# A11 B11 of a feed-forward kernel's second matrix product made by seven quarter products, from the third unit on

## The chip, the cores and the metric

The kernel runs on one core of a Trainium2 chip. The metric is the device time of one execution in microseconds (us), as the median of several runs. The kernel before took 959.35 us (median of 3 runs, 957.83 to 960.07). The profiled execution spans 957.3 us, and all positions in the traces are microseconds from the start of that span.

## The reference, cut to what matters

```python
kv  = einsum('bhsd,bhse->bhde', k, v)             # linear attention, 8 x 8 heads, 576 x 64
o   = einsum('bhsd,bhde->bhse', q, kv)
o   = o / sqrt(mean(o*o, -1) + 1e-6) * g_norm
x   = o.transpose(0, 2, 1, 3).reshape(4608, 512)
h   = x @ w_in                                    # 512 -> 2048
g   = s * relu(h)**2 + b
out = g @ w_out                                   # 2048 -> 512
```

All of it is fp32. The change touches only the last line, `g @ w_out`. The kernel keeps r = relu(h)**2 as its hidden value and puts the rest into the evacuation: the result is s * (r @ w_out) plus one constant row, the column sums of w_out times b (`b_row`, line 329, whose left and right halves are `b1` and `b2`).

## The kernel before, in words

The 4608 tokens are worked in nine units of 512 tokens (`u` = 0 to 8; the loop is at line 1152). In a unit comes first the **first product** (`mm1`, line 562), which gives the hidden values transposed, in four steps `s` = 0 to 3 of 4 x 128 hidden rows, and then the **second product** (`mm2`, line 646). Beside the second product, the attention of the next unit's tokens is made in small pieces (`turn`, `product`, `norm`, `turn_x`, lines 388 to 472).

Both products use a scheme with seven block products in place of eight (Winograd's form of Strassen's). A matrix is cut into four blocks; products 1 to 7 are made of blocks and of sums of blocks, and the partial results are added. In the second product the hidden values are A (`a11`: first 256 tokens, first half of the hidden rows; `a12`: the same tokens, second half; `a21` and `a22`: the other 256 tokens), and w_out is B (512-column rows cut into halves of 256). A11 B11 is product 1, A12 B21 is product 2, and so on (`G_OF`, line 644, tells which A goes with which number).

A plain block product (`product`, line 650) runs for each of two 128-token groups `j` over 8 hidden blocks `f`: each call is one matmul with 128 x 128 weights and 256 columns, accumulated in a PSUM bank. In the traces one fp32 call is two weight loads and two matmul records, so such a product has 16 records for each `j`.

From the third unit on (`u` > 1), three of the seven, products 2, 7 and 4 (`TWICE`, line 274), are made by the scheme **a second time** (`second_level`, line 678): the block is cut again, into quarters, and seven quarter products of 4 calls each (8 records) with 128 columns stand for the plain product's two groups. They need four sums of quarters of A, made on VectorE (`sums`, line 688), and the sums of quarters of B, which are made once, in unit 1 (`parts_of_w`, line 664), stored in HBM (`w3_dram`, line 275) and loaded again in each unit.

The quarter products run in the order 1, 2, 6, 7, 5, 3, 4 (`ORDER`, line 618). They share PSUM banks, and the way they do is needed below. Quarter product 1 starts the bank called "x" (line 716); `keep` (line 711) reads it on VectorE into a small tile `r1`; then product 6 **adds to the same bank** (line 724), `r2` is read from it, and product 5 adds to it again (line 731), then product 3. Product 7 starts the bank "y", and product 4 adds to it. Product 2 has the bank "z".

PSUM pool `ps_f` has two banks with the tag "x", two with the tag "y" and one "z". In `second_level` both "x" and "y" are taken from the tag "y" (line 704).

The order of the work is written out by hand: the program runs under a manual schedule (line 87), so each engine runs its instructions in the order in which the Python code issues them. For `u` > 1 that order is in `first` (line 924) and `second` (line 929). Around the end of the first product it is: `x5` of step 3 (its bank is copied by ScalarE, then VectorE adds and squares it: line 590), then `first` (two transposes `turn`, and `x1(0)`, half of product 1), then the last two blocks of the first product, `x3` and `y4` of step 3 (lines 1197 to 1199), then `second`: two of the four sums for product 2, `x1(1)`, and the quarter products of product 2. `attend(0)` (line 920) is the attention product of the next unit's first 128 tokens with its norm, and `x6_of(0)` (line 896) the next plain product; it reads `a11` after `s2` (line 798) has overwritten it with a sum.

Weights of the second product come through a ring of seven tiles (`late["ring"]`, line 997), loaded on SyncE's queue by `pump` (line 628), two tiles a call.

Of the kernel before, what the change touches and what calls it, by code (L numbers as in the profile page):

```python
# [15 lines left out]
def kernel(  # L16
# [211 lines left out]
    def add(o, a, b):  # L228
        nc.vector.tensor_tensor(out=o, in0=a, in1=b, op=ALU.add)  # L229
# [41 lines left out]


    w2_dram = [dram.tile([P, FC // 2, HN], FP32, name=f"w2_{i}") for i in range(8)]
    TWICE = (2, 7, 4)
    w3_dram = {
        i: dram.tile([P, 7, FC // 4, P], FP32, name=f"w3_{i}") for i in TWICE
    }
# [232 lines left out]
    def bank_of(key, tag, bufs=2):  # L510
        bank[key] = ps_f.tile([P, 2, TB], FP32, name=f"{tag}_ps", tag=tag, bufs=bufs)
        return bank[key]
# [133 lines left out]
    def mm2(u, att=None):  # L646
# [3 lines left out]
        def product(i, j, ps, first):  # L650
            for f in range(FC // 2):
                s, b = divmod(f, 2)
                w2 = W2_AT[i][:, f] if u == 0 else ring[u, i, f // 4][:, f % 4]
                matmul(
                    ps, ga[G_OF[i], s][:, b, j * P : j * P + P], w2,
                    first and f == 0, f == FC // 2 - 1,
                )

        def scaled(o, ps, other):
            nc.vector.scalar_tensor_tensor(o, ps, s_col, other, ALU.mult, ALU.add)  # L660
# [14 lines left out]
            for n, t in enumerate((y11, y21, t2, t3, t1, y22, t4)):  # L675
                nc.sync.dma_start(out=w3_dram[i][:, n], in_=t)

        def second_level(i, other, to):


            a, t, r = {}, {}, {}
            cols = [slice(q * P, q * P + P) for q in range(2)]

            def quarter(j, h):
                g = g_pair[G_OF[i], h].rearrange("p s b t -> p (s b) t")
                return g[:, :, j * P : j * P + P]

            def sums(which=(5, 6, 7, 3)):
                x11, x12, x21, x22 = (quarter(j, h) for j in range(2) for h in range(2))
                a.update({1: x11, 2: x12, 4: x22})  # L690
                for m in which:
                    a[m] = late["sub"].tile([P, FC // 4, P], FP32, name="sub", tag="sub")
                    if m == 5:
                        add(a[5], x21, x22)
                    elif m == 6:
                        sub(a[6], a[5], x11)
                    elif m == 7:
                        sub(a[7], x11, x21)
                    else:
                        sub(a[3], x12, a[6])  # L700

            def go(m, bank, first):
                if first:
                    t[bank] = bank_of((bank, i), "z" if bank == "z" else "y", 1 if bank == "z" else 2)
                    t[bank] = t[bank].rearrange("p b n -> p (b n)")[:, :P]
                n = ORDER.index(m)
                w = ring[u, i, n // 2][:, n % 2]
                for f in range(FC // 4):
                    matmul(t[bank], a[m][:, f], w[:, f], first and f == 0, f == FC // 4 - 1)

            def keep(name, j, q):
                r[name] = late["tmp"].tile([P, P], FP32, name="r", tag="r")
                scaled(r[name], t["x"], other(j, cols[q]))

            def m1():
                go(1, "x", True)
                keep("r1", 0, 0)

            def m2():
                go(2, "z", True)  # L720
                scaled(to(0, cols[0]), t["z"], r["r1"])

            def m6():
                go(6, "x", False)
                keep("r2", 1, 0)

            def m7():
                go(7, "y", True)

            def m5():  # L730
                go(5, "x", False)
                keep("r4", 1, 1)
                scaled(to(1, cols[1]), t["y"], r["r4"])

            def m3():
                go(3, "x", False)
                scaled(to(0, cols[1]), t["x"], other(0, cols[1]))

            def m4():
                go(4, "y", False)  # L740
                scaled(to(1, cols[0]), t["y"], r["r2"])

            return {"sums": sums, 1: m1, 2: m2, 6: m6, 7: m7, 5: m5, 3: m3, 4: m4}
# [7 lines left out]
        def rows(name, j):  # L751
            if (name, j) not in st:
                st[name, j] = outp.tile([P, DM], FP32, name=name, tag=name)
            return st[name, j]
# [15 lines left out]
        def x1(j):  # L770
            st["x", j] = half(("x", j), "x")
            product(1, j, st["x", j], True)
            if u > 0:
                part("r1", j, st["x", j], b1)
# [49 lines left out]

        def x3(j):
            product(3, j, st["x", j], False)
            scaled(rows("o1", j)[:, HN:], st["x", j], b2 if u > 0 else st["o1", j][:, HN:])
            store("o1", j, 4 * u + j)

        def y4(j):  # L830
# [40 lines left out]
            ]  # L871
        if u == 1:
            return [
                lambda: x1(0),
                seq(lambda: x1(1), lambda: pump(2), s2),
                seq(lambda: z2(0), lambda: parts_of_w(2)),
                seq(lambda: z2(1), lambda: pump(2), s4),
                lambda: x6(0),
                seq(lambda: x6(1), lambda: pump(2)),
                seq(lambda: y7(0), lambda: parts_of_w(7)),  # L880
                seq(lambda: y7(1), lambda: pump(2)),
                lambda: x5(0),
                seq(lambda: x5(1), lambda: pump(2)),
                lambda: x3(0),
                seq(lambda: x3(1), lambda: pump(2)),
                seq(lambda: y4(0), lambda: parts_of_w(4)),
                seq(lambda: y4(1), lambda: pump(2)),
            ]

        p2 = second_level(2, lambda j, q: st["r1", j][:, q], lambda j, q: rows("o1", j)[:, q])  # L890
        p7 = second_level(
            7, lambda j, q: b2[:, q], lambda j, q: rows("o2", j)[:, HN:][:, q]
        )
        p4 = second_level(4, lambda j, q: st["r2", j][:, q], lambda j, q: rows("o2", j)[:, q])

        def x6_of(j):
            product(6, j, st["x", j], False)
            part("r2", j, st["x", j], b_12)

        def x5_of(j):  # L900
# [1 line left out]

        def with_7(j):

            right = st["o2", j][:, HN:]
            add(st["r2", j], st["r2", j], right)
            scaled(right, st["x", j], right)
            if last(j):
                store("o2", j, 4 * u + 2 + j, slice(HN, DM))

# [10 lines left out]
            product_q[c]()  # L921
            norm[c]()

        def first():
            turn[0]()
            turn[1]()
            x1(0)

        def second():
            p2["sums"]((5, 6))  # L930
            x1(1)
            pump(2)
            p2[1]()
            p2["sums"]((7,))
            p2[2]()
            p2["sums"]((3,))
            p2[6]()
            s2((0, 1))
            p2[7]()
            p2[5]()  # L940
            s2((2, 3))
            pump(2)
            attend(0)
            p7["sums"]()
            x6_of(0)
            p2[3]()
            p2[4]()
            pump(2)
            attend(1)
            turn_x[0]()  # L950
            turn[2]()
            x6_of(1)
            pump(2)
            p7[1]()
            s4((0,))
            p7[2]()
            p7[6]()
            s4((1,))
            p7[7]()
            s4((2,))  # L960
            p7[5]()
            s4((3,))
            pump(2)
            attend(2)
            turn_x[1]()
            turn[3]()
            x5_of(0)
            p7[3]()
            with_7(0)
            p7[4]()  # L970
            pump(2)
            attend(3)
            turn_x[2]()
            x5_of(1)
            with_7(1)
            turn_x[3]()
            pump(2)
            p4["sums"]()
            x3(0)
            for m in (1, 2, 6, 7, 5):  # L980
                p4[m]()
            pump(2)
            x_sums_next[0]()
            x3(1)
            pump(2)
            y4_of(0, 3)
            y4_of(1, 4)
            pump(2)

        return [first, second]  # L990


    NU = FC // 2
# [158 lines left out]
    for u in range(U):  # L1152
# [11 lines left out]
            slots += [a["x6"], a["y7"], a["x5"]]  # L1164
        if u == 0:
            first_unit()
        for n, slot in enumerate(slots):
            slot()
            if u == 1 and n in (1, 3, 5):
                for sums in sums_w_in((n + 1) // 2):  # L1170
                    sums()
            if u in kv_due and n == 12:
                kv_product(kv_due[u])
            elif u + 1 in kv_due and n == 14:
                for i in range(2):
                    load_kv(kv_due[u + 1], i, late["kv"], tag="kv")
        side = side_of(u)
        second = mm2(u, side if u > 1 else None)
        if u > 1:
            side = {}  # L1180
        for n, slot in enumerate(second):
# [55 lines left out]
```

## Time and profile before

| | busy us | share of the 957.3 us |
|---|---|---|
| TensorE matmuls (PE) | 944.8 | 99% |
| TensorE weight loads (PEld, beside the matmuls) | 839.6 | 88% |
| VectorE (DVE) | 580.6 | 61% |
| ScalarE (ACT) | 194.5 | 20% |
| DMA, all queues | 143.73 MB moved, 150 GB/s | |

The granted TensorE clock is 0.997 over the span. Units 2 to 8 are alike and take about 102 us each: `x1(0)` starts at 294.42, 396.43 and so on.

How to read the profile: a row of a timeline has a start, a duration, the engine, the line of the kernel, the operation, the tile written and the tiles read, and the shape. Several instructions in a row that are alike are merged and counted (x16). Line 90 is the matmul helper, so tiles tell the products apart: `x_ps`, `y_ps` and `z_ps` are the banks, `w_sb` the ring of weights, `a` any hidden block, `sub` a sum for the second level. A merged PE row lasts until its last matmul has drained; the pace is the distance from its start to the start of the next row. Idle time of an engine that is not the bound costs nothing.

### The profile page before, as it was taken

What the parts mean: (1) busy time and instruction counts of PE and PEld (TensorE: products, weight loads), DVE (VectorE), ACT (ScalarE), POOL (GpSimd) and SP (SyncE); (2) the same over time, 40 slices, a digit from 0 to 9 for tenths busy, and PEclk for the clock granted to TensorE, in tenths of its full rate; (3) what the DMA queues carried; (4) which work ended last, traced back from release to release, by engine and by line L of the source; (5) the groups of instructions that cost most, each with busy time, mean ns of one, the idle gap of its engine ahead of it and who ended that gap; (6) DMA issues with size and microseconds to landing.
All of it is one profiled execution on the core that took longest, in us unless ns stands there. A gap on an engine that the chain in (4) does not pass through costs nothing.

```text
span 957.3 us, 16744 instructions
## 1 busy us (share of the span) xinstructions
PE 944.8 (99%) x6934; PEld 839.6 (88%) x6934; DVE 580.6 (61%) x1019; ACT 194.5 (20%) x366; POOL 6.7 (1%) x18
## 2 busy tenths in 40 slices
PE   7999999999999999999999999999999999999997
PEld 7888888888888898899889988989898988998897
DVE  2789667465537754586358745774467556864463
ACT  2684131201120112112211212021202111111100
POOL 2000000000000000000000000000000000000000
PEclk9999999999999999999999999999999999999999
DMA  9598729567743565165444565266215630552063
GB/s 240 193 323 242 256 78 278 110 186 215 209 98 101 180 185 120 45 203 161 111 107 152 169 167 117 91 197 180 31 59 180 194 64 19 191 175 68 1 207 101
DMA packets 127532, 143.73 MB, mean 150 GB/s; under 512 B 76256, under 2 KB 87264, under 8 KB 127328
## 3 DMA queue, kind: packets, MB, share of 16 engines
q1 hardware_dynamic: 124352, 140.88, 51.3%
q10 hardware_dynamic: 2784, 1.77, 0.8%
q8 instruction: 55, 0.90, 0.4%
q14 instruction: 21, 0.17, 0.1%
q0 software_dynamic: 320, 0.00, 0.0%
HBM read 120.33 MB, written 22.28 MB: 149 GB/s over the span
## 4 chain that ended last, share of the span: by engine, by line
PE 96%; DMA 2%; DVE 1%; ACT 1%; issue 0%; SPq 0%; ACTq 0%; DVEq 0%
PE x_ps L90 51%; PE y_ps L90 30%; PE z_ps L90 8%; PE x_ps L421 3%; PE kv_ps L359 2%; DMA w_raw<-in_moe_w_in_dram 1%; DMA kv_sb<-in_k_dram 1%; PE qT_ps L400 0%; DVE xn L440 0%; DVE xT L464 0%; ACT xT L470 0%; ACT w_raw L209 0%; SPq L102 0%; ACT w_raw L204 0%; DVE wb L224 0%
## 5 line engine op out<-in xcount | busy, mean ns | idle before, releaser
L90 PE MATMUL x_ps<-w_sb,a 128*128 128x256 f32 x768 | 174.7, 381 | 0.0
L90 PEld LDWEIGHTS x_ps<-w_sb,a 128*128 128x128 f32 x768 | 144.0, 190 | 21.5 <-issue 2.8
L568 ACT COPY r<-x_ps 128x512 f32<-128x512 f32 x96 | 56.2, 585 | 332.0 <-PE x_ps L90 325.3
L90 PE MATMUL y_ps<-xs,wb 128*128 128x256 f32 x512 | 121.0, 379 | 0.0
L90 PE MATMUL x_ps<-xs,ws 128*128 128x256 f32 x512 | 120.9, 379 | 0.0
L229 DVE TENSOR_TENSOR a<-y_ps,r 128x512 f32<-128x512 f32 x64 | 44.0, 688 | 122.2 <-ACT r L568 122.2
L90 PEld LDWEIGHTS x_ps<-xs,ws 128*128 128x128 f32 x512 | 97.3, 190 | 13.2
L90 PEld LDWEIGHTS y_ps<-xs,wb 128*128 128x128 f32 x512 | 97.3, 190 | 13.2
L90 PE MATMUL x_ps<-xT,wa 128*128 128x256 f32 x384 | 89.6, 380 | 0.1
L90 PE MATMUL y_ps<-w_sb,sub 128*128 128x128 f32 x672 | 81.8, 275 | 0.0
L90 PEld LDWEIGHTS x_ps<-xT,wa 128*128 128x128 f32 x384 | 72.3, 190 | 10.2 <-ACT xT L470 0.5
L90 PEld LDWEIGHTS y_ps<-w_sb,sub 128*128 128x128 f32 x672 | 80.0, 192 | 1.1
L523 DVE SCALAR_TENSOR_TENSOR a<-a 128x512 f32<-128x512 f32 x96 | 66.5, 692 | 3.3
L601 DVE TENSOR_TENSOR a<-a 128x512 f32<-128x512 f32 x32 | 22.1, 691 | 75.9 <-ACT a L600 75.9
L90 PE MATMUL y_ps<-w_sb,a 128*128 128x128 f32 (+1 forms) x416 | 62.2, 295 | 0.0
L90 PE MATMUL x_ps<-xT,ws 128*128 128x256 f32 x256 | 61.1, 381 | 0.0
L90 PE MATMUL z_ps<-xT,wa 128*128 128x256 f32 x256 | 60.5, 379 | 0.0
L90 PEld LDWEIGHTS y_ps<-w_sb,a 128*128 128x128 f32 x416 | 57.5, 191 | 3.2 <-issue 0.2
L90 PE MATMUL x_ps<-w_sb,s 128*128 128x256 f32 x256 | 59.1, 384 | 0.0
L90 PEld LDWEIGHTS x_ps<-w_sb,s 128*128 128x128 f32 x256 | 47.4, 190 | 8.4 <-issue 2.4
L430 ACT ACTIVATE xn<-x_ps 128x512 f32<-128x512 f32 x34 | 20.3, 597 | 168.4 <-PE x_ps L421 165.9
L90 PEld LDWEIGHTS z_ps<-xT,wa 128*128 128x128 f32 x256 | 48.6, 190 | 6.6
(122 smaller groups left out, 994.9 us busy)
## 6 DMA issues: line engine op xcount, KB each, us to landing
w_sb<-w SPq DMA_DIRECT2D x133, 512.0 KB, 4.7
kv_sb<-in_k_dram SPq DMA_DIRECT2D x30, 288.0 KB, 5.3
kv_sb<-in_v_dram SPq DMA_DIRECT2D x30, 288.0 KB, 6.1
w_raw<-in_moe_w_in_dram SPq DMA_DIRECT2D x8, 1024.0 KB, 7.2
w_raw<-in_moe_w_out_dram SPq DMA_DIRECT2D x8, 1024.0 KB, 5.3
out_dram<-o SPq DMA_DIRECT2D x104, 64.0 KB, 1.7
w_sb<-w SPq DMA_DIRECT2D x21, 256.0 KB, 2.8
q_sb<-in_q_dram SPq DMA_DIRECT2D x144, 32.0 KB, 2.1
```

Source lines behind the costliest of these rows:

```text
L90: nc.tensor.matmul(o, lhsT=lhsT, rhs=rhs, start=start, stop=stop, skip_group_check=True)
L229: nc.vector.tensor_tensor(out=o, in0=a, in1=b, op=ALU.add)
L359: nc.tensor.matmul(ps[r][l * HB : l * HB + HB, i, :], lhsT=kv[rows, 0, l, j, :], rhs=kv[rows, 1, l, j, :], start=(j == 0), stop=(j == R - 1),)
L421: nc.tensor.matmul(ps[32 * p : 32 * p + 32, w, :], lhsT=st["qT"][:, p, 32 * w : 32 * w + 32], rhs=bd_kv[(b if w < 2 else b1) % 2][:, p, :] ...
L430: nc.scalar.activation(st["xn"], st["x"], AF.Square)
L523: nc.vector.scalar_tensor_tensor(t, t, 0.0, t, ALU.max, ALU.mult)
L568: nc.scalar.copy(st[name], src)
L601: nc.vector.tensor_mul(t, t, t)
```

## The change

Product 1 joins `TWICE`: from the third unit on, A11 B11 too is made of seven quarter products. Its purpose is to make that product with fewer multiplications on TensorE. The quarter products 1, 2, 6, 7 and 5 stand before the last two blocks (`x3`, `y4`) of the first product, and 3 and 4 after them; the four sums are issued ahead of `x5` of the last step.

Because A11 B11 is then no longer in a PSUM bank that products 6, 5 and 3 could add to, it is kept (with `b2`) in the right half of the output rows `o1`, and goes from there into the evacuations of products 2, 7 and 3. Product 6 starts its own bank, and the left half of the rows gets `b_12` = `b1` - `b2` by two more additions. The attention product of the next unit (`product_q[0]`) moves ahead of product 2's quarter products, and its norm stays behind them.

```diff
-    TWICE = (2, 7, 4)
+    TWICE = (1, 2, 7, 4)
@@ second_level
-        def second_level(i, other, to):
+        def second_level(i, other, to, x_tag="y"):
...
-                    t[bank] = bank_of((bank, i), "z" if bank == "z" else "y", 1 if bank == "z" else 2)
+                    tag = {"x": x_tag}.get(bank, bank)
+                    t[bank] = bank_of((bank, i), tag, 1 if tag == "z" else 2)
@@ x3
-            scaled(rows("o1", j)[:, HN:], st["x", j], b2 if u > 0 else st["o1", j][:, HN:])
+            scaled(rows("o1", j)[:, HN:], st["x", j], b2 if u == 1 else st["o1", j][:, HN:])
@@ unit 1
-                lambda: x1(0),
+                seq(lambda: x1(0), lambda: parts_of_w(1)),
@@ units 2 to 8
+        def right(name, j, q=slice(0, HN)):
+            return rows(name, j)[:, HN:][:, q]
+
-        p2 = second_level(2, lambda j, q: st["r1", j][:, q], lambda j, q: rows("o1", j)[:, q])
+        p1 = second_level(1, lambda j, q: b2[:, q], lambda j, q: right("o1", j, q), "x")
+        p2 = second_level(2, lambda j, q: right("o1", j, q), lambda j, q: rows("o1", j)[:, q])
...
-            7, lambda j, q: b2[:, q], lambda j, q: rows("o2", j)[:, HN:][:, q]
+            7, lambda j, q: right("o1", j, q), lambda j, q: right("o2", j, q)
...
         def x6_of(j):
-            product(6, j, st["x", j], False)
+            st["x", j] = half(("x", j), "x")
+            product(6, j, st["x", j], True)
...
-        def first():
+        def sums_ahead():
+            p1["sums"]()
             turn[0]()
             turn[1]()
-            x1(0)
+
+        def first():
+            for m in (1, 2, 6, 7, 5):
+                p1[m]()
+            pump(2)
 
         def second():
+            p1[3]()
             p2["sums"]((5, 6))
-            x1(1)
+            p1[4]()
             pump(2)
+            product_q[0]()
             p2[1]()
             p2["sums"]((7,))
             p2[2]()
...
-            attend(0)
+            norm[0]()
             p7["sums"]()
             x6_of(0)
             p2[3]()
             p2[4]()
+            for j in range(2):
+                left = rows("o1", j)[:, :HN]
+                add(left, left, b_12)
@@ the loop over the units
+        side = side_of(u)
+        second = mm2(u, side if u > 1 else None)
+        if u > 1:
+            ahead, *second = second
         for n, slot in enumerate(slots):
             slot()
+            if u > 1 and n == len(slots) - 2:
+                ahead()
```

More of the change, by code (lines that the diff above doesn't have):

```diff
@@ L903, in with_7 @@
         def with_7(j):
-            right = st["o2", j][:, HN:]
-            add(st["r2", j], st["r2", j], right)
-            scaled(right, st["x", j], right)
+            to = right("o2", j)
+            add(st["r2", j], st["r2", j], to)
+            scaled(to, st["x", j], to)
             if last(j):
@@ L988, in second @@
             pump(2)
-        return [first, second]
+        return [sums_ahead, first, second]
     NU = FC // 2
@@ L1176 @@
                     load_kv(kv_due[u + 1], i, late["kv"], tag="kv")
-        side = side_of(u)
-        second = mm2(u, side if u > 1 else None)
         if u > 1:
```

## The prediction

> **What bounds the kernel now.** I read the page's busy table first, then the chain that ended last:
>
> ```profile
> PE 944.8 (99%) x6934; PEld 839.6 (88%) x6934; DVE 580.6 (61%) x1019; ACT 194.5 (20%) x366; POOL 6.7 (1%) x18
> ```
> ```profile
> PE 96%; DMA 2%; DVE 1%; ACT 1%; issue 0%; SPq 0%; ACTq 0%; DVEq 0%
> ```
>
> TensorE sets the time; nothing else is within a third of it on average. Where TensorE isn't held up, a change is worth its matmul time; an idle gap made on TensorE is paid in full. So I looked at the seam that the change rebuilds, in the timeline of unit 3 (start, duration, engine):
>
> ```profile
> 394.70 1.89 PE L90 MATMUL x_ps<-xs,ws 128*128 128x256 f32 x8
> 396.43 3.62 PE L90 MATMUL x_ps<-w_sb,a 128*128 128x256 f32 x16
> 396.68 0.59 ACT L568 COPY r<-x_ps 128x512 f32<-128x512 f32 x1 [2.92 <-PE x_ps L90]
> 397.30 0.69 DVE L229 TENSOR_TENSOR a<-y_ps,r 128x512 f32<-128x512 f32 x1 [3.88 <-ACT r L568]
> 398.03 0.69 DVE L523 SCALAR_TENSOR_TENSOR a<-a 128x512 f32<-128x512 f32 x1
> 398.63 1.30 DVE L391 STREAM_TRANSPOSE qT<-q_sb 128x512 f32<-128x512 f32 x2
> 399.88 1.89 PE L90 MATMUL x_ps<-xT,ws 128*128 128x256 f32 x8
> 401.61 1.89 PE L90 MATMUL y_ps<-xs,wb 128*128 128x256 f32 x8
> ...
> 403.33 3.62 PE L90 MATMUL x_ps<-w_sb,a 128*128 128x256 f32 x16
> ...
> 405.21 0.69 DVE L523 SCALAR_TENSOR_TENSOR a<-a 128x512 f32<-128x512 f32 x1
> ...
> 405.94 0.69 DVE L229 TENSOR_TENSOR sub<-a,a 128x512 f32<-128x512 f32 x1
> 406.67 0.69 DVE L232 TENSOR_TENSOR sub<-sub,a 128x512 f32<-128x512 f32 x1
> 406.79 1.05 PE L90 MATMUL y_ps<-w_sb,a 128*128 128x128 f32 x8
> ...
> 407.27 0.48 DVE L660 SCALAR_TENSOR_TENSOR or<-x_ps,s_col,b_row 128x256 f32<-128x256 f32 x1
> 407.68 1.06 PE L90 MATMUL z_ps<-w_sb,a 128*128 128x128 f32 x8
> 407.88 0.35 DVE L660 SCALAR_TENSOR_TENSOR r<-y_ps,s_col,or 128x128 f32<-128x128 f32 x1
> 408.15 0.68 DVE L232 TENSOR_TENSOR sub<-a 128x512 f32<-128x512 f32 x1
> 408.57 2.84 PE L90 MATMUL y_ps<-w_sb,sub 128*128 128x128 f32 x24
> ```
>
> In order: `x5` of the last step (394.70), `x1(0)`, `x3`, `y4` (401.61), `x1(1)` (403.33), then quarter products 1, 2 and 6, 7, 5 of product 2. Two things are to be seen. TensorE never pauses. And VectorE, 61% busy on average, works without a pause from 404.5 on: r1, read from bank "x", ends at 408.23, only 0.34 before quarter product 6 adds to that bank (408.57).
>
> [...] The rows agree: both engines keep the code's order. So a late evacuation stops the matmul that needs its bank and all matmuls behind it. [...] here the data alone forces it, since r1 must be read before 6 is added. [...] this trace has 690. [...] here 350, which I use.
>
> **The change, part by part.**
>
> *Matmul work.* 16 records of 256 columns take 3.45 (396.43 to 399.88), so `x1(0)` and `x1(1)` cost 6.90. In their place come 56 records of 128 columns. In product 2, 8 take 0.89 or 0.90 (406.79, 407.68, 408.57), hence 56 take 6.26. Saved: 0.64 a unit, in seven units 4.5 us. That is all there is to gain.
>
> *VectorE order.* A started 128x512 operation holds the next one back 0.60 (0.73 if the next needs its result), a 128x128 one 0.27 (0.39). PSUM is readable 0.20 after the next TensorE row begins (401.61, ScalarE's 401.81). VectorE's end reaches TensorE's weight load 0.06 later (near the start a copy ends at 24.65, the load is at 24.71); from its restart a matmul may lose 0 to 0.2 more.
>
> *First wait, quarter product 6 of product 1.* I keep unit 3's clock. Products 1 and 2 run 396.43 to 398.22, where 6 wants bank "x". It must wait for r1, which stands on VectorE behind the evacuation of `x5`: ScalarE's copy ends 397.27, the add is at 397.30, the square at 398.03, so r1 starts 398.63 and ends 398.98. Moving the sums ahead doesn't help, since it is ScalarE's copy that the add waits for. (The four sums and two transposes start about 393.35 and end about 397.2, in the 3.88 that VectorE idles now: no cost.) Product 6 starts about 399.09, a wait of 0.87; bounds 0.80 and 1.0. Behind it stand all of TensorE's matmuls. Before, `x1(0)` covered this: 3.45 of matmul that needed nothing from VectorE.
>
> *`x3`, `y4`.* r2 and r4 then follow in time; ScalarE's and VectorE's work on `x3` and `y4` keeps its distance to them. Call the end of `y4` Y (403.33 before). The square of `y4` starts at Y+1.88, as before.
>
> *Second wait, quarter product 6 of product 2.* TensorE after Y: 3 and 4 of product 1 (1.79), the attention product (0.1 to switch, 1.01), quarter products 1 and 2 (1.79): 6 is wanted at Y+4.68; before it came at Y+5.24. VectorE from the square: evacuation of 3 at Y+2.48, two sums at 2.75 and 3.48, evacuation of 4 at 4.08, the attention's row sum of squares at 4.35, r1 at 4.98, done at 5.33. Product 6 starts about Y+5.40: a wait of 0.72, bounds 0.65 and 0.9. The sum for 7 ends at 5.93, in time for Y+6.3. TensorE's path has become 0.56 shorter and VectorE's row before r1 0.78 longer (r1 began at Y+4.55, waiting 0.13 for its turn).
>
> *Third.* `x6_of(0)` now follows directly, without the attention product's 1.01 as cover. It starts Y+8.1 and needs the third block of `s2` at Y+9.8; this is done at Y+9.62. With the weight load ahead that is 0 to 0.25; I take 0.1.
>
> *A unit:* 0.87 + 0.72 + 0.1 - 0.64 = +1.05; six units (2 to 7): +6.3.
>
> *The last unit* has no attention. Product 6 of product 2 is wanted at Y+3.6 and r1, without the row sum before it, ends at 4.70: 1.15, with some 0.05 for a bank that `y4`'s add frees at Y+1.85. 0.87 + 1.2 - 0.64 = +1.4.
>
> *Costed at nothing:* the weights of product 1 in unit 1 (four VectorE operations, 2.7; VectorE idles there before 196.00 and again before 200.55, and `z2` needs their followers after 203), their seven stores (like those of product 2, in the next 3 to 6 us, and the two ring slots are wanted again only for `x6`, 10 us later), the larger loads (4 tiles for 2; four quarter tiles of product 1 arrive during the 45 us of the first product; 512 KB land in 4.7 and the tightest, the second tile of `x6`, has about 8), and the two additions by `b_12` (0.8, under `x6_of(1)`). Banks of `x6_of` are long free.
>
> Sum: 959.35 + 6.3 + 1.4 = 967.0.
>
> **The rivals.** *A, as above:* 967.0; low bounds (0.80 + 0.65 - 0.64 = 0.8 a unit, 1.2 in the last) give 965.3, high ones (1.0 + 0.9 + 0.25 - 0.64 = 1.5, last 1.9) 970.3.
>
> *B, the matmuls decide (faster):* the evacuations keep up and 4.5 is saved: 954.9. For it: products 2, 7 and 4 run by this scheme with no pause now. Against it: in products 7 and 4, VectorE had caught up when they began; here both r1 stand behind a full row of 128x512 work.
>
> *C, one wait only:* the first or the second is hidden by something that I mis-ordered. Then a unit gives -0.64 + 0.1 + 0.72 or 0.87, so +0.2 to +0.3: over seven units 960.6 to 961.7.
>
> *D, more waits:* VectorE stays behind into product 7, or a ring tile is late. In my row r1 of product 7 is still waiting for TensorE, 0.3 ahead of need. 0.7 more a unit: 972.
>
> **How the numbers follow.** A 0.77, B 0.09, C 0.08, D 0.06. The likeliest gives 967.0. The range takes A's bounds and the runs' own spread of 1 us: 964 to 971. Faster by over 0.2% (1.9 us): B, and a little for a case in which both waits shrink, 0.10. Within: most of C, 0.06. Slower: the rest, 0.84.
>
> **What would show it.** In the profile after: a hole of about 0.9 in TensorE's row before the 24 records of quarter products 6, 7, 5 of product 1, ended by VectorE's r (line of `scaled`), and one of about 0.7 before those of product 2, ended likewise; in the last unit 1.1 there. 56 records of 128 columns in 6.26 apart from the holes. The four sums ahead of `x5` without cost. Wrong it would be if product 6 ran on at once (then r1 was read earlier than I order it), if the holes lay elsewhere, or if the matmuls' pace differed from product 2's.

## The result, and the profile after

The changed kernel took 964.85 us (median of 6 runs, 964.15 to 966.49) against 958.59 us of the kernel before in the same comparison: a ratio of 1.0064, with a 95% interval of 1.0045 to 1.0082. (Ratios below are formed in the same way, each against the kernel before as it ran beside that version.) It is slower by 6.3 us, less than 1% but clear of the noise. The two profiled executions span 964.3 and 957.3 us. The forecast was 967.0 us, 7.65 us slower than the 959.35 us known then.

The page of the changed kernel, its line of busy times:

```profile
PE 943.5 (98%) x7102; PEld 840.8 (87%) x7102; DVE 612.1 (63%) x1100; ACT 194.3 (20%) x366; POOL 6.7 (1%) x18
```

TensorE has 168 records more (7 units, 56 for 32) and a little less busy time (944.8 us before), and yet the span is longer: the time went into gaps. VectorE has 31.5 us more work. The view of the waits tells who made the gaps (engine and what it wrote, whom it waited for, us in total, times, longest):

```profile
PEld x_ps L90 <- DVE r L660: 6.0, 7, 0.9
...
PE x_ps L90 <- DVE r L660: 4.6, 7, 0.7
PEld y_ps L90 <- DVE r L660: 4.4, 7, 1.0
...
PE y_ps L90 <- DVE r L660: 3.1, 7, 0.8
```

None of these four is in the waits of the kernel before. Each comes seven times, once in each of units 2 to 8: TensorE waits for the tile `r`, an evacuation by VectorE, once before it writes bank "x" and once before bank "y". The timeline of unit 3 shows the first of the two, at the place that answers to 394.70 to 403.33 before (unit 3 starts 1.2 us later in this execution):

```profile
395.88 1.89 PE L90 MATMUL x_ps<-xs,ws 128*128 128x256 f32 x8
...
397.61 1.05 PE L90 MATMUL x_ps<-w_sb,a 128*128 128x128 f32 x8
397.87 0.58 ACT L568 COPY r<-x_ps 128x512 f32<-128x512 f32 x1 [2.92 <-PE x_ps L90]
...
398.49 0.69 DVE L229 TENSOR_TENSOR a<-y_ps,r 128x512 f32<-128x512 f32 x1
398.50 1.06 PE L90 MATMUL z_ps<-w_sb,a 128*128 128x128 f32 x8
399.21 0.69 DVE L523 SCALAR_TENSOR_TENSOR a<-a 128x512 f32<-128x512 f32 x1
...
399.82 0.34 DVE L660 SCALAR_TENSOR_TENSOR r<-x_ps,s_col,b_row 128x128 f32<-128x128 f32 x1
...
400.22 1.16 PE L90 MATMUL x_ps<-w_sb,sub 128*128 128x128 f32 x8 [0.66 <-DVE r L660]
...
401.22 1.06 PE L90 MATMUL y_ps<-w_sb,sub 128*128 128x128 f32 x8
```

Quarter product 1 starts at 397.61, 2 at 398.50; 6 was due 0.89 later, at 399.39, and starts at 400.22, after r1, which VectorE could begin only at 399.82, behind the copy, add and square of `x5`. The row's own 0.66 is counted from the modelled end of the matmuls before; the start is late by 0.83.

The second, at the head of product 2 (the 32 records of line 421 are the attention product):

```profile
408.34 1.08 PE L421 MATMUL x_ps<-bd_kv,qT 128*32 128x128 f32 x32
...
409.35 1.16 PE L90 MATMUL y_ps<-w_sb,a 128*128 128x128 f32 x8
...
410.34 1.06 PE L90 MATMUL z_ps<-w_sb,a 128*128 128x128 f32 x8
...
410.80 0.68 DVE L432 TENSOR_REDUCE ss<-xn 128x8 f32<-128x512 f32 x1
411.39 0.34 DVE L660 SCALAR_TENSOR_TENSOR r<-y_ps,s_col,o 128x128 f32<-128x128 f32 x1
...
411.79 2.94 PE L90 MATMUL y_ps<-w_sb,sub 128*128 128x128 f32 x24 [0.39 <-DVE r L660]
...
414.57 3.62 PE L90 MATMUL x_ps<-w_sb,a 128*128 128x256 f32 x16
...
418.02 1.05 PE L90 MATMUL y_ps<-w_sb,sub 128*128 128x128 f32 x8
```

Due at 411.23, started at 411.79: 0.56 late, behind r1, which here stands behind the row sum of squares of the attention (410.80).

Each of units 2 to 7 became 0.93 us longer: quarter product 1 of unit 2 starts 0.26 later than `x1(0)` did (294.68 for 294.42), that of unit 8 5.81 later (907.39 for 901.58), which is 5.55 over six units. The last unit became 1.55 longer. With the 0.26 from before unit 2, and 0.4 won back behind the last matmuls, where the stores end, this is the 7.0 between the spans.

### The profile page after: what moved, and what is told of

It reads as the page before. It is cut to its first block, busy times and chain, and to the rows that moved or that the text cites. A ratio compares the mean times of both kernels' runs of the same rounds, so it can differ in the third digit from the quotient of the medians.

```text
span 964.3 us, 17222 instructions
## 1 busy us (share of the span) xinstructions
PE 943.5 (98%) x7102; PEld 840.8 (87%) x7102; DVE 612.1 (63%) x1100; ACT 194.3 (20%) x366; POOL 6.7 (1%) x18
## 5 line engine op out<-in xcount | busy, mean ns | idle before, releaser
L90 PE MATMUL x_ps<-w_sb,a 128*128 128x256 f32 (+1 forms) x600 | 130.9, 371 | 0.0
L90 PEld LDWEIGHTS x_ps<-w_sb,a 128*128 128x128 f32 x600 | 108.6, 190 | 15.2 <-issue 1.6
L90 PE MATMUL y_ps<-w_sb,sub 128*128 128x128 f32 x728 | 90.0, 276 | 3.1 <-DVE r L660 3.1
L90 PEld LDWEIGHTS y_ps<-w_sb,sub 128*128 128x128 f32 x728 | 86.8, 192 | 5.5 <-DVE r L660 4.4
L90 PEld LDWEIGHTS x_ps<-xT,wa 128*128 128x128 f32 x384 | 72.3, 190 | 10.2 <-ACT xT L470 0.5
L90 PE MATMUL y_ps<-w_sb,a 128*128 128x128 f32 (+1 forms) x472 | 70.3, 294 | 0.0
L90 PEld LDWEIGHTS y_ps<-w_sb,a 128*128 128x128 f32 x472 | 63.8, 191 | 4.2 <-DVE o L660 1.2
L90 PEld LDWEIGHTS x_ps<-xT,ws 128*128 128x128 f32 x256 | 47.6, 190 | 6.3
```

The lines of the kernel that those rows point to most:

```text
L90: nc.tensor.matmul(o, lhsT=lhsT, rhs=rhs, start=start, stop=stop, skip_group_check=True)
```

## The experiments

The theory at this point: the matmul work fell as forecast, and two separate waits for an evacuation, each placed late in VectorE's order of work (r1 at 399.82 behind the square at 399.21, and at 411.39 behind the row sum at 410.80), cost more. The rival that is hard to tell apart from a trace: VectorE as a whole is the bound of this stretch (its pauses between 406 and 424 are few and short in either kernel, none above 0.8 us), and a gap that is closed opens again further on.

**The first wait alone.** Quarter product 1, and with it r1, goes ahead of `x5`; 6 comes before 2, so that r2 is not delayed in turn. Nothing is left out.

```diff
         def sums_ahead():
             p1["sums"]()
+            p1[1]()
             turn[0]()
...
-            for m in (1, 2, 6, 7, 5):
+            for m in (6, 2, 7, 5):
                 p1[m]()
```

> Edit: quarter product 1 of A11 B11 and its evacuation r1 are issued before x5 of the first product (after the four sums), and the rest runs 6, 2, 7, 5; only the order changes. Theory (two separate waits for evacuations that stand late on VectorE): r1 is read before the evacuation of x5, so the hole of 0.82 us before quarter product 6 of product 1 and about 0.1 for the restart go away in seven units, 6.4 us in all: about 958.4 us, with the second hole (0.56 in units 2 to 7, 0.97 in the last) as it was. Rival (VectorE as a whole is the bound of the seam, and a hole closed opens again further on): about 964.5 us as in the changed kernel, the second hole grown to about 1.4.

Measured: 958.11 us (13 runs), ratio to the kernel before 0.9998 (0.9990 to 1.0006). That is what the theory gave (958.4). Its timeline of unit 3:

```profile
394.31 1.05 PE L90 MATMUL x_ps<-w_sb,a 128*128 128x128 f32 x8
...
395.20 1.89 PE L90 MATMUL x_ps<-xs,ws 128*128 128x256 f32 x8
395.48 0.34 DVE L660 SCALAR_TENSOR_TENSOR r<-x_ps,s_col,b_row 128x128 f32<-128x128 f32 x1
...
396.93 1.05 PE L90 MATMUL x_ps<-w_sb,sub 128*128 128x128 f32 x8
```

and its row of the second wait:

```profile
PE y_ps L90 <- DVE r L660: 3.1, 7, 0.8
```

r1 is done at 395.82, more than a microsecond before 6 needs its bank (396.93), and no gap is left there. The second wait is as it was, in sum (3.1) and in its longest (0.8). So the first wait did not move on. Its cost was 6.3 us by the two ratios (1.0064 less 0.9998, each known to 0.1 or 0.2%), and by the trace of the changed kernel 7 x 0.94 = 6.6 (0.83 late and 0.11 for the restart, the first step after the gap taking 1.00 where the others take 0.89). That is as much as the whole slowdown: the saving of matmul work and the second wait are left, and nearly cancel.

**The second wait alone.** The row sum of squares is split from the attention product (`False` leaves it to a later call; the lines that define `sum_sq_of` are not shown) and issued by `sum_sq_of` after the sums of `s2`. Nothing is left out. The helper's line 660 is line 667 in this version and the later ones with it.

```diff
-            product_q[0]()
+            product_q[0](False)
             p2[1]()
...
             s2((2, 3))
             pump(2)
+            if att:
+                sum_sq_of[4 * u + 4]()
             norm[0]()
```

> Edit: the attention product stays where it is, but its row sum of squares on VectorE (0.68 us) is issued behind the second pair of s2 sums instead of ahead of r1 of product 2. Theory: r1 of product 2 ends 0.63 us earlier, the hole of 0.56 before quarter product 6 of product 2 closes in units 2 to 7 (with its restart 0.6 to 0.7 each, 4 us in all): about 961 us; the last unit, without attention, keeps its 0.97. Rival (VectorE as a whole is the bound): the hole opens again before x6 or in product 7, about 964.5 us.

Measured: 963.94 us (5 runs), ratio to before 1.0057 (1.0045 to 1.0069); 0.7 less than the changed kernel by the ratios and 1.4 by the profiled spans (962.9 for 964.3), where the theory gave 4. The two intervals overlap, so the trace has to tell what happened. Here the theory fell short. Its timeline of unit 3:

```profile
410.35 0.34 DVE L667 SCALAR_TENSOR_TENSOR r<-y_ps,s_col,o 128x128 f32<-128x128 f32 x1
...
410.78 2.90 PE L90 MATMUL y_ps<-w_sb,sub 128*128 128x128 f32 x24
...
424.31 1.06 PE L90 MATMUL z_ps<-w_sb,a 128*128 128x128 f32 x8
...
425.12 0.34 DVE L667 SCALAR_TENSOR_TENSOR r<-y_ps,s_col,o 128x128 f32<-128x128 f32 x1
...
425.50 1.64 PEld L90 LDWEIGHTS y_ps<-w_sb,sub 128*128 128x128 f32 x14 [0.33 <-DVE r L667]
```

The gap of product 2 is closed (410.78), but a new one stands 15 us later, before quarter product 6 of **product 7**: due at 425.20, it starts at 425.50, again after an r1. VectorE had carried its backlog that far: of the 0.66 won in a unit (0.56 and about 0.1 of restart) 0.4 was given back.

**Both.** The two edits together.

> Edits of the two runs before together. Theory: both holes go and the matmul saving of 0.64 us a unit is left, less about 0.8 in the last unit: about 954.5 us, faster than the kernel before by 4 us (0.4%). Rival (VectorE as a whole is the bound): little under 962 us, with new holes further on, first before quarter product 6 of product 7.

Measured: 956.77 us (14 runs), ratio to before 0.9991 (0.9982 to 0.9999). Its view of waits has one row for the gaps that `r` makes:

```profile
PEld y_ps L90 <- DVE r L667: 2.9, 7, 1.0
```

In units 2 to 7 the two early gaps are gone and product 7's is there, with 0.31 and its restart of 0.1; the longest, 1.0, is the second gap of the last unit, which has no row sum to move. 6 x 0.41 = 2.5 us, and the 954.5 of the theory with 2.5 is 957.0, close to what was measured. So both theories hold in part: the first wait was a matter of order alone, the second one hid a true backlog of VectorE, of less than half a microsecond, which ended at product 7.

**The backlog taken away.** The two additions of `b_12`, 0.75 us together, stood right in that backlog; they are needed only when the rows are stored. From the version with both edits they move to behind quarter product 4 of product 7, where VectorE idled 1.03 us in the kernel before (434.17 to 435.20).

```diff
             p2[4]()
-            for j in range(2):
-                left = rows("o1", j)[:, :HN]
-                add(left, left, b_12)
...
             p7[4]()
+            for j in range(2):
+                left = rows("o1", j)[:, :HN]
+                add(left, left, b_12)
```

> Edit: as in the run with both edits, and the two additions of b_12 (0.75 us on VectorE) are issued behind quarter product 4 of product 7, where VectorE idled 1.03 us in the kernel before, instead of ahead of the second attention product. Theory: the hole of 0.31 us that the two edits left before quarter product 6 of product 7 is made by VectorE's backlog there, and r1 of product 7 comes 0.4 to 0.6 us earlier: it closes, with its restart 0.4 us in each of six units: 956.8 - 2.4 = 954.4 us; only the last unit keeps its hole of 0.97. Rival (VectorE's backlog moves on once more): about 956.8 us with a hole further on.

Measured: 955.33 us (13 runs), ratio to before 0.9966 (0.9957 to 0.9975). This version beats both kernels: by medians it is 2.7 us under the 958.02 of the kernel before beside it, by the ratio 3.3. Of the gaps made by `r` one is left in its view of waits, that of the last unit:

```profile
PEld y_ps L90 <- DVE r L667: 1.0, 1, 1.0
...
PE y_ps L90 <- DVE r L667: 0.8, 1, 0.8
```

**One sum more out of the way.** The sum for quarter product 7 of product 2 needs no block of the last step; on top of the edit before, it is issued before `x3`, where VectorE idled 1.6 us in the version with both edits (399.22 to 400.84).

```diff
             for m in (6, 2, 7, 5):
                 p1[m]()
+            p2["sums"]((7,))
...
             p2[1]()
-            p2["sums"]((7,))
             p2[2]()
```

> Edit: as in the run with the additions later, and the sum for quarter product 7 of product 2, which needs only blocks of the first two steps, is issued before the last two blocks of the first product, where VectorE idles 1.6 us. Theory: no hole was left there in units 2 to 7, so nothing is gained: as the run with the additions later, about 954.4 us; r1 in the last unit stands ahead of this sum already, so its hole of 0.97 stays. Rival (VectorE's total work between y4 and product 7 is the bound): another 0.6 us a unit less, about 951 us.

Measured: 955.03 us (5 runs), ratio to before 0.9967 (0.9954 to 0.9979), the same as without it. VectorE's total work is no longer the bound there; of the rival nothing more was to be had.

**The first wait made longer.** The four sums go behind `x5`'s evacuation, where they would stand if `sums_ahead` didn't exist.

```diff
         def sums_ahead():
-            p1["sums"]()
             turn[0]()
             turn[1]()

         def first():
+            p1["sums"]()
             for m in (1, 2, 6, 7, 5):
```

> Edit: the four sums of product 1 are issued behind x5's evacuation instead of ahead of it, everything else as in the changed kernel (the suspected wait made longer by a known amount). Theory: r1 stands behind four more operations of 0.60 to 0.73 us, 2.6 us in all, and the first hole grows from 0.82 to about 3.4 in each of seven units: 964.9 + 18 = 983 us. Rival (the hole is the bank or the loads, not VectorE's queue): about 965 us.

Measured: 992.03 us (2 runs, 989.42 and 994.64), 9 more than expected, and a ratio of 1.0353 (1.0326 to 1.0380). The row of this gap in its view of waits, and units 3 and 4 of its timeline (TensorE only):

```profile
PE x_ps L90 <- DVE r L660: 22.3, 7, 3.2
...
404.74 1.16 PE L90 MATMUL x_ps<-w_sb,sub 128*128 128x128 f32 x8 [3.19 <-DVE r L660]
...
407.52 1.89 PE L90 MATMUL x_ps<-xT,ws 128*128 128x256 f32 x8
...
510.21 2.07 PE L90 MATMUL x_ps<-w_sb,sub 128*128 128x128 f32 x8 [3.19 <-DVE r L660]
512.07 1.92 PE L90 MATMUL y_ps<-w_sb,sub 128*128 128x128 f32 x8
513.78 1.91 PE L90 MATMUL x_ps<-w_sb,sub 128*128 128x128 f32 x8
515.49 2.15 PE L90 MATMUL x_ps<-xT,ws 128*128 128x256 f32 x8
```

The gap is 3.19 in the row in all seven units, 3.36 by the starts, as expected (3.4): the wait follows VectorE's queue, not the bank or the loads, for neither of which anything was changed. That is 17.7 us (22.3 for 4.6 in the view of waits). The rest lies behind the gaps. In unit 3 the 24 records after it take 2.78 (404.74 to 407.52), in unit 4 5.28 (510.21 to 515.49): the matmuls run at half their pace for 5 us. The section on the hardware returns to this.

## Why the prediction was right

*What bounds the kernel.* Right: a gap on TensorE was paid in full, as the run without the first one shows (6.6 us of gap and restart by the trace, 6.3 by the ratios). The chain of unit 3 from quarter product 1 (before, `x1(0)`) to `x6_of(0)` grew from 15.93 us (396.43 to 412.36) to 16.96 (397.61 to 414.57), by 1.03 for a forecast 0.95 (0.87 + 0.72 - 0.64). `x6_of(0)` itself, forecast 0.1 longer, became 0.1 shorter; that makes the unit 0.93 longer for a forecast 1.05.

*Matmul work.* 0.64 a unit was forecast. No time that the profile shows contradicts it: without restart the 8-record steps are 0.89 or 0.90 apart, as taken from product 2.

*The first wait.* The order of work behind it was right to the start of r1 (398.63 forecast in the old clock, 399.82 measured, 1.19 later, of which 1.18 is the later start of the unit). The gap was put at 0.87 and is 0.83; the restart, which the forecast left between 0 and 0.2 and then took as 0, costs 0.11 (the first step after the gap is 400.22 to 401.22). Together 0.94. That without it there is no loss is shown by the first experiment.

*The second wait.* 0.72 was forecast; it is 0.56 and 0.1 of restart. The term that was off is TensorE's side: quarter product 2 starts 0.99 after 1, not 0.89, since the first matmuls after the attention product took 0.1 more (409.35 to 410.34), which the sum counted once, ahead of it, and not again behind it. And r1 ended 5.27 after `y4`, not 5.33. A side remark was wrong, though nothing in the sum rests on it: VectorE's row before r1 was not to grow by 0.78, which sets r1's end (5.33) against its old start (4.55), but by 0.43 from start to start (4.98), and grew by 0.38 (411.39 is 4.93 after `y4`). A 128x128 operation was costed at the 350 ns that the trace before shows, and r1 takes 0.34 again.

*The third wait*, 0.1 before the third block of `s2`: it isn't there. `x6_of(0)` runs its 16 records in 3.45 (414.57 to 418.02), and no longer pays the 0.1 that it had to pay before, when it followed the attention product and took 3.55:

```profile
411.35 1.08 PE L421 MATMUL x_ps<-bd_kv,qT 128*32 128x128 f32 x32
412.36 3.72 PE L90 MATMUL x_ps<-w_sb,a 128*128 128x256 f32 x16
415.91 1.05 PE L90 MATMUL y_ps<-w_sb,sub 128*128 128x128 f32 x8
```

The errors in a unit go both ways and partly cancel: +0.07 in the first wait, -0.06 in the second, +0.1 behind the attention product, -0.1 for the third wait and -0.1 in `x6_of(0)`. To that extent the closeness of 0.93 to 1.05 is luck.

*The last unit.* 1.4 forecast, 1.55 in the trace.

*What was costed at nothing* cost nothing in the changed kernel: unit 1's weight sums, their stores and the larger loads (TensorE's rows from 185 to 209 start 0.26 later throughout, with no gap between them), the four sums ahead of `x5`, and the two additions. The last held only because the second gap gave VectorE time: once it was closed, the additions stood in the way.

*The rivals.* B, that the evacuations keep up, is what the order with all three edits does, but for the last unit, whose gap stays: it saves 2.7 us by medians and 3.3 by the ratio, for a forecast 4.5. The saving was there to be had. D, a backlog that reaches product 7, was right in kind, though not for this kernel: it appears only when the second gap is closed. That VectorE and TensorE keep the order of the code, on which the case rested, is in every row shown here: r1 (399.82) comes behind the square (399.21), and no matmul row passes quarter product 6 while it waits (400.22, the next at 401.22).

## What to carry to other kernels

Splitting a long accumulation into short ones that share a bank turns work that needs nothing from another engine into work that depends on an evacuation about every microsecond (a quarter product takes 0.89). Whether that cost anything was here a matter of order: 6.3 us with r1 behind `x5`, and no gap with r1 ahead of it. Ask, for each short product, what stands ahead of its evacuation in the queue of the engine that does it. Pulling operands ahead did not help where the read that must come *between* two accumulations stayed behind (the four sums stood ahead of `x5`, and the gap was 0.83); move the product and its read together. And close gaps one after the other with a trace in between, since a gap can hide how little slack the helper engine has behind it, as product 7 showed.

## What the runs showed of the hardware that was not expected

In the run with the late sums, four of the seven gaps of 3.2 us on TensorE cost more than themselves: they were followed by matmuls at half pace; the 24 records took 4.29, 5.28, 4.39 and 4.41 us in units 2, 4, 5 and 8, and 2.78 in units 3, 6 and 7, though the gaps were equal (3.19 in the rows, 3.36 by the starts). This table of stretches around unit 4's gap shows the clock (stretch and length in us; busy us and instructions of matmuls, weight loads, VectorE, ScalarE and GpSimd; then the granted TensorE clock, the DMA share and GB/s):

```profile
505.00:510.20 5.20, 2.01 (x18) 1.80 (x16) 4.14 (x7) 0.59 (x1) 0.00 (x0) 0.90 1.06 229
510.20:515.40 5.20, 5.19 (x24) 5.20 (x25) 0.70 (x2) 0.00 (x0) 0.00 (x0) 0.50 0.18 50
515.40:520.00 4.60, 4.60 (x26) 4.12 (x25) 2.33 (x5) 0.60 (x1) 0.00 (x0) 0.94 0.27 99
```

The clock is 0.50 for the 5.2 us after the gap and comes back by itself. Wider stretches of the same trace, from units 3, 4 and 5, give the length of the low clock:

```profile
398.00:404.70 6.70, 3.55 (x25) 3.15 (x23) 4.14 (x7) 0.59 (x1) 0.00 (x0) 1.00 0.14 39
404.70:411.00 6.30, 6.26 (x41) 5.85 (x42) 2.29 (x6) 0.60 (x1) 0.00 (x0) 1.00 0.26 86
500.00:510.20 10.20, 7.01 (x41) 6.20 (x39) 7.35 (x13) 1.17 (x2) 0.00 (x0) 0.95 1.04 235
510.20:515.50 5.30, 5.29 (x25) 5.30 (x26) 0.70 (x2) 0.00 (x0) 0.00 (x0) 0.50 0.18 53
515.50:517.50 2.00, 2.00 (x10) 1.73 (x10) 0.70 (x2) 0.00 (x0) 0.00 (x0) 0.88 0.60 215
610.00:622.00 12.00, 8.81 (x49) 8.21 (x49) 6.34 (x12) 1.17 (x2) 0.00 (x0) 0.86 0.22 54
```

An estimate, with 0.50 as the low value and 1.00 as the other: in unit 4 it lasts 1.0 (0.05 x 10.2 / 0.5) + 5.3 + 0.5 (0.12 x 2.0 / 0.5) = 6.8 us, of which 1.0 lies ahead of the matmuls' restart at 510.21; in unit 5 3.4 us (0.14 x 12 / 0.5). In unit 3, with the same gap, the clock is 1.00 throughout. In unit 8 the half pace sets in only behind the restart: the first 8 records take 1.06 (931.51 to 932.57), the next 8 1.71:

```profile
931.51 1.27 PE L90 MATMUL x_ps<-w_sb,sub 128*128 128x128 f32 x8 [3.19 <-DVE r L660]
932.57 1.92 PE L90 MATMUL y_ps<-w_sb,sub 128*128 128x128 f32 x8
934.28 1.80 PE L90 MATMUL x_ps<-w_sb,sub 128*128 128x128 f32 x8
```

So the length of a gap alone did not decide whether the clock fell. The start of the kernel before and of the changed kernel shows the same: here is the row behind the longest of TensorE's gaps between 20 and 30 us, first before, then after.

```profile
22.60 0.63 PE L458 MATMUL xT_ps<-ident,xn 128*128 128x128 f32 x4 [1.81 <-ACT w_raw L209]
```
```profile
23.01 0.63 PE L458 MATMUL xT_ps<-ident,xn 128*128 128x128 f32 x4 [2.11 <-ACT w_raw L209]
```

Behind the gap of 1.81 the clock is 0.50 from about 23.3 to 26.7; behind the longer one, of 2.11, it stays at 1.00. What decides it, none of these runs shows.

The four slow stretches sum to 7.5 us (1.5 + 2.75 + 1.6 + 1.6, with the start of unit 4's `x3`); with the 17.7 of the gaps that is 25.2, less 2.0 by which this execution reached unit 2 earlier, and the spans differ by 23.2. The other run of this version is 5.2 us longer at a lower mean clock (0.985 for 0.991), as it would be if the clock had fallen behind more of its gaps; of that run there is no trace. The gaps of the changed kernel in units 2 to 8, under 1 us, show nothing of the kind: the clock is 1.00 around all of them, and from the second step behind the first gap on the pace is again 0.89 for 8 records.
